# Reciprocal denominators spread by bf16 selection matmuls, with gated loads and a new order of preparation, in a fused linear-attention and MLP kernel

## The chip, the cores and the metric

The kernel runs on one core of one Trainium2 chip. The time is device microseconds (us) of that core, as the median of several executions. The kernel before takes 422 us. A profile shows one execution; its span (first to last instruction) is some 2 us below the time of that execution. The profile of the kernel before is of an execution of 419.1 us, 3 us faster than its median. TensorE's clock is granted in steps: the profile calls full speed 1.00, and half speed is 0.50.

## The reference, cut to what matters

```python
# B, H, S, D = 8, 8, 576, 64
def phi(x, c, s):                       # c, s = cos, sin of (pi/2) * position / S
    r = np.maximum(x, 0.0)
    return np.concatenate([r * c, r * s], axis=-1)
q_p, k_p = phi(q, cos_w, sin_w), phi(k, cos_w, sin_w)
kv  = einsum('bhsf,bhsd->bhfd', k_p, v)
z   = sum(k_p, axis=2)
num = einsum('bhsf,bhfd->bhsd', q_p, kv)
den = einsum('bhsf,bhf->bhs', q_p, z)[..., None] + 1e-06
attn = num / den
# tokens to rows: x is [4608, 512]
h = x @ w_in                            # 512 -> 2048
g = h / (1 + exp(-1.702 * h))
out = g @ w_out                         # 2048 -> 512
```

## The kernel before: the parts the argument touches

The MLP works on nine blocks of 512 tokens. A block has 32 units: 16 of the first matmul (`mm1`, four matmuls 128x512 and a gelu on ScalarE), then 16 of the second (`mm2`, four matmuls 128x512). Attention of the next batch (576 tokens) is slipped in between the units. Attention of one batch is: relu of q, k; transposed q times cos and sin; `kv`; `den`; a reciprocal per token and head; spreading it over the 64 partitions of the head's outputs ("the spread"); `num` times the spread reciprocals, into `xT`, which is the MLP's input.

The reciprocals `inv` lie in 32 rows of a head pair: row `32j + 16hh + 4g` holds head `2j+hh` and token segment `g`, and each value is repeated in four rows. There are two ways to spread them. Batches 0 and 1 use fp32 matmuls with a 0/1 selection matrix; batches 2 to 7 go through DRAM:

```python
def spread_dma(b):
    scr = dram.tile([2, NP, NSEG, SEG], F32, name="scr")
    for hh in range(2):
        for j in range(NP):                                  # eight small stores
            nc.gpsimd.dma_start(out=scr[hh, j], in_=s["inv"][32*j+16*hh : 32*j+16*hh+16 : 4])
    for hh in range(2):                                      # two broadcast loads
        nc.gpsimd.dma_start(out=s["invb"][hh*64:hh*64+64]..., in_=scr[hh]....to_broadcast([64, NP*S]))

def spread_pe(b, j):
    for hf in range(2):
        bps = ps.tile([128, TB], F32, name="yps", bufs=2)
        for g2 in range(2):
            nc.tensor.matmul(bps[:, ds(g2*SEG, SEG)], sel[32*j:32*j+32, 2*hf+g2]..., # fp32
                             s["inv"][32*j:32*j+32, :], start=True, stop=True)
        nc.scalar.copy(s["invb"][:, j, ds(hf*HF, HF)], bps[:, 0:HF])
...
# block i > 1; b1 = i+1 is finished here, b2 = i+2 is prepared here
for j in range(NP): work[j].append(unit_kv(b1, j))
work[6].append(unit_den(b1)); work[6].append(spread_dma(b1))
for j in range(NP):
    for hf in range(2): work[min(24 + 2*j + hf, 32)].append(unit_num(b1, j, hf))
for n, f in zip(range(8, 30), prep_all(b2)): work[n].append(f)     # relu, DMA transposes, v, trig
work[20].append(load_all(b2 + 1))
```

In the opening the queries of batch 0 are transposed by five DMA transposes, the weights' loads are issued when K has landed, and all heads of batch 0 go through each step together.

Of the kernel before, what the change touches and what calls it, by code (L numbers as in the profile page):

```python
# [15 lines left out]
EQ = mybir.AluOpType.is_equal  # L16
PSUM = bass.MemoryType.PSUM
DRAM = bass.MemoryType.DRAM
# [3 lines left out]
def kernel(  # L22
# [25 lines left out]
    dram = ctx.enter_context(tc.tile_pool(name="dram", bufs=2, space=DRAM))  # L48
# [6 lines left out]
    nc.gpsimd.memset(warm, 0.0)  # L55
    for _ in range(56):
        wps = ps.tile([128, TB], F32, name="hps", bufs=2)
        nc.tensor.matmul(wps, warm[:, 0:128], warm, start=True, stop=True)  # L58

    def load(src, b, name):  # L60
        t = one.tile([128, 2560], F32, name=name)
        nc.sync.dma_start(
            out=t[:, 0:2048].rearrange("p (h e) -> p h e", h=H),
            in_=src[b, :, 0:512, :].rearrange("h (p c) d -> p h (c d)", c=4))
        nc.sync.dma_start(  # L65
            out=t[0:64, 2048:2560].rearrange("p (h d) -> p h d", h=H),
            in_=src[b, :, 512:576, :].rearrange("h p d -> p h d"))
        return t

    def chunk(t, c):  # L70
        if c < 4:
            return t[:, 0:2048].rearrange("p (j hh c d) -> p c j hh d", hh=2, c=4, d=D)[:, c]
        return t[0:64, 2048:2560].rearrange("p (j hh d) -> p j hh d", hh=2, d=D)

    def slots(t):
        return t[:, 0:2048].rearrange("p (h c d) -> p h c d", c=4, d=D)

    state = {b: {} for b in range(B)}
    for name, src in (("qf", q), ("kf", k), ("vf", v)):
        state[0][name] = load(src, 0, name)  # L80
# [7 lines left out]
    eps = const.tile([128, 1], F32)  # L88
    nc.vector.memset(eps, 1e-6)
# [5 lines left out]
    nc.gpsimd.iota(col_i[:, 512:576], pattern=[[1, 64]], base=512, channel_multiplier=0)  # L95
    pos_f = const.tile([128, 5], F32)
    nc.vector.tensor_copy(pos_f, pos_i)
    col_f = tpool.tile([128, S], F32)
    nc.vector.tensor_copy(col_f, col_i)
    sinw = const.tile([128, 5], F32)  # L100
# [9 lines left out]
    nc.vector.memset(mask_z, 0.0)  # L110
    for hh in range(2):
        nc.vector.memset(mask_n[hh * 64:hh * 64 + 64, :, hh * 64:hh * 64 + 64], 1.0)
        for s in range(NSEG):
            nc.vector.memset(mask_z[hh * 64:hh * 64 + 64, s, hh, s, :], 1.0)
    sel_i = tpool.tile([128, NSEG, 2, 64], I32)
    sel = const.tile([128, NSEG, 2, 64], F32)
# [3 lines left out]
    nc.vector.tensor_scalar(sel, sel_i, 0.0, None, op0=EQ)  # L120

    tmp.close()
    gpool = ctx.enter_context(tc.tile_pool(name="gpool", bufs=19))
    ypool = ctx.enter_context(tc.tile_pool(name="ypool", bufs=3))

    krs, vts = [], []
    for i in range(2):
        kr = one.tile([128, 5, NP, 128], BF16, name=f"kr{i}")
        vt = one.tile([128, 5, NP, VW], BF16, name=f"vt{i}")
        nc.gpsimd.memset(kr[64:128, 4], 0.0)  # L130
        nc.gpsimd.memset(vt[64:128, 4], 0.0)
        for c in range(5):
            np_ = 128 if c < 4 else 64
            for cs, w in enumerate((cosw, sinw)):
                nc.gpsimd.tensor_copy(
                    vt[:np_, c, :, 256 + cs:257 + cs],
                    w[:np_, c:c + 1].unsqueeze(1).to_broadcast([np_, NP, 1]))
        krs.append(kr)
        vts.append(vt)
# [8 lines left out]
    def prep_q(b):  # L148
        s = state[b]
        qn = one.tile([128, 5, H, D], BF16, name="qn")  # L150
        s["qTr"] = one.tile([128, NP, S], BF16, name="qTr")
        if b == 0:
            for c in range(4):
                nc.vector.tensor_scalar(qn[:, c], slots(s["qf"])[:, :, c], 0.0, None, op0=MAX)
        else:
            nc.vector.tensor_scalar(qn[:, 0:4].rearrange("p c h d -> p h c d"), slots(s["qf"]), 0.0, None, op0=MAX)
        nc.vector.tensor_scalar(qn[0:64, 4].rearrange("p h d -> p (h d)"), s["qf"][0:64, 2048:2560], 0.0, None, op0=MAX)
        for c in range(5):
            np_ = 128 if c < 4 else 64
            nc.sync.dma_start_transpose(out=s["qTr"][:, :, c * 128:c * 128 + np_],  # L160
                                        in_=qn[:np_, c].rearrange("p h d -> p (h d)"))

    def prep_k(b):
        s = state[b]
        s["kr"] = kr = krs[b % 2]
        if b == 0:
            nc.scalar.activation(kr[:, 0:4].rearrange("p c j (hh d) -> p (j hh) c d", hh=2), slots(s["kf"]), AF.Relu)
            nc.scalar.activation(kr[0:64, 4].rearrange("p j e -> p (j e)"), s["kf"][0:64, 2048:2560], AF.Relu)
        else:
            for c2 in range(2):  # L170
                nc.vector.tensor_scalar(
                    kr[:, 2 * c2:2 * c2 + 2].rearrange("p c j (hh d) -> p (j hh) c d", hh=2),
                    slots(s["kf"])[:, :, 2 * c2:2 * c2 + 2], 0.0, None, op0=MAX)
            nc.vector.tensor_scalar(kr[0:64, 4].rearrange("p j e -> p (j e)"), s["kf"][0:64, 2048:2560], 0.0, None,
                                    op0=MAX)

    def prep_v(b, c):
        s = state[b]
        s["vt"] = vt = vts[b % 2]
        np_ = 128 if c < 4 else 64  # L180
        for cs, w in enumerate((cosw, sinw)):
            o = vt[:np_, c, :, cs * 128:cs * 128 + 128].rearrange("p j (hh d) -> p j hh d", hh=2)
            if b == 0 and cs == 1 and c in (1, 2, 3):
                nc.scalar.activation(o, chunk(s["vf"], c), AF.Identity, scale=w[:np_, c:c + 1])
            else:
                nc.vector.tensor_scalar(o, chunk(s["vf"], c), w[:np_, c:c + 1], None, op0=MUL)  # L186

    def prep_trig(b, j):
        s = state[b]
        if j == 0:  # L190
            s["qT"] = two.tile([128, NP, 2, S], BF16, name="qT")
        for cs in range(2):
            nc.vector.tensor_tensor(s["qT"][:, j, cs, :], s["qTr"][:, j, :], trig[:, cs, :], op=MUL)  # L193


    def unit_kv(b, j):
        s = state[b]
        kv_ps = ps.tile([128, VW], F32, name="kv_ps")
        for c in range(5):
            nc.tensor.matmul(kv_ps, s["kr"][:, c, j, :], s["vt"][:, c, j, :],  # L200
                             start=(c == 0), stop=(c == 4))
        kvs = two.tile([128, 2, 128], BF16, name="kvs", bufs=6)
        zs = two.tile([128, 2, NSEG, 32], BF16, name="zs", bufs=5)
# [7 lines left out]
    def unit_den(b):  # L211

        s = state[b]
        den_ps = ps.tile([128, SEG], F32, name="den_ps")
        for g in range(NSEG):
            for cs in range(2):
                for j in range(NP):
                    nc.tensor.matmul(den_ps[32 * j:32 * j + 32, :], s["zs"][j][:, cs, g, :],  # L218
                                     s["qT"][:, j, cs, ds(g * SEG, SEG)],
                                     start=(g == 0 and cs == 0), stop=(g == NSEG - 1 and cs == 1))  # L220
        den = two.tile([128, SEG], F32, name="den", bufs=1)
        nc.scalar.activation(den, den_ps, AF.Identity, bias=eps)  # L222
        inv = two.tile([128, SEG], F32, name="inv", bufs=1)
        nc.vector.reciprocal(inv, den)  # L224
        s["inv"] = inv
        s["invb"] = two.tile([128, NP, S], F32, name="invb", bufs=1)

    def spread_dma(b):
        s = state[b]
        scr = dram.tile([2, NP, NSEG, SEG], F32, name="scr")  # L230
        for hh in range(2):
            for j in range(NP):
                nc.gpsimd.dma_start(out=scr[hh, j], in_=s["inv"][32 * j + 16 * hh:32 * j + 16 * hh + 16:4])  # L233
        for hh in range(2):
            nc.gpsimd.dma_start(
                out=s["invb"][hh * 64:hh * 64 + 64].rearrange("p j s -> p (j s)"),
                in_=scr[hh].rearrange("j g s -> (j g s)").unsqueeze(0).to_broadcast([64, NP * S]))

    def spread_pe(b, j):
        s = state[b]  # L240
        for hf in range(2):
            bps = ps.tile([128, TB], F32, name="yps", bufs=2)
            for g2 in range(2):
                nc.tensor.matmul(bps[:, ds(g2 * SEG, SEG)],  # L244
                                 sel[32 * j:32 * j + 32, 2 * hf + g2].rearrange("p hh d -> p (hh d)"),
                                 s["inv"][32 * j:32 * j + 32, :], start=True, stop=True)
            nc.scalar.copy(s["invb"][:, j, ds(hf * HF, HF)], bps[:, 0:HF])  # L247

    def unit_num(b, j, hf):
        s = state[b]  # L250
        num_ps = ps.tile([128, HF], F32, name="num_ps", bufs=2)
        for cs in range(2):
            nc.tensor.matmul(num_ps, s["kvs"][j][:, cs, :], s["qT"][:, j, cs, ds(hf * HF, HF)],  # L253
                             start=(cs == 0), stop=(cs == 1))
        nc.vector.tensor_tensor(xT[:, j, ds(b * S + hf * HF, HF)], num_ps,  # L255
                                s["invb"][:, j, ds(hf * HF, HF)], op=MUL)
# [65 lines left out]
    for c in range(5):  # L322
        prep_v(0, c)
# [90 lines left out]
```

## Time and profile before

| stage (first MLP matmul to first MLP matmul) | us |
|---|---|
| opening, up to block 0's first MLP matmul | 52.4 |
| blocks 0, 1, 2, 3, 4, 5, 6 | 46.1, 53.5, 45.2, 44.4, 43.7, 38.3, 32.8 |
| blocks 7, 8 (no attention left) and the tail | 60.8 |

The borders are read from the timeline of TensorE.

The page's first part, of the kernel before: busy time of each engine, share of the span, instructions.

```profile
PE 339.3 (81%) x1785; PEld 166.3 (40%) x1816; DVE 142.5 (34%) x334; ACT 124.8 (30%) x215; POOL 73.6 (18%) x106
```

TensorE looks nearly full here. By stage it is not. The window table of the kernel before follows: stretch, its length, busy time of each engine with its number of instructions, granted TensorE clock, mean share of the DMA engines and GB/s.

```profile
core 0: us, PE busy (x) PEld busy (x) DVE busy (x) ACT busy (x) POOL busy (x), PEclk, DMA share, GB/s
0.00:52.40 52.40, 34.07 (x156) 18.72 (x158) 19.39 (x54) 10.97 (x19) 16.99 (x46) 0.68 1.06 227
...
98.50:152.00 53.50, 35.24 (x192) 16.77 (x195) 26.54 (x62) 11.90 (x21) 8.75 (x10) 0.82 0.75 187
...
197.30:241.70 44.40, 34.43 (x195) 16.63 (x197) 17.59 (x40) 12.31 (x22) 10.71 (x10) 0.88 0.57 144
...
323.60:356.50 32.90, 32.69 (x194) 16.14 (x196) 7.74 (x17) 12.18 (x22) 5.00 (x10) 1.00 0.30 69
```

Block 3 (third row) and block 6 (fourth) do the same TensorE work, 195 and 194 matmuls. Block 6 needs 32.9 us and is full; block 3 takes 44.4 us and leaves TensorE 10 us idle. The waits of the kernel before (who waited for whom: us in all, times, longest) name the cause:

```profile
DVE xT L255 <- DMA invb<-scr: 62.0, 5, 16.6
...
PE num_ps L253 <- DVE xT L255: 50.3, 5, 18.1
```

The chain of waits through block 3 (start, us, what) shows the way of the reciprocals:

```profile
207.36 1.06 DVE inv L224
...
208.71 8.43 POOL scr L233 x6
...
217.88 6.80 DMA scr<-inv
...
225.23 8.65 DMA invb<-scr
...
234.01 0.47 DVE xT L255
...
234.52 0.64 PE num_ps L253 x2
```

The reciprocal is done at 208.4, and num goes on at 234.5: 26.1 us for one trip through DRAM. When its num buffers are full TensorE stands still, and the MLP matmuls that come later in its program stand with it: in the last 7.2 us of the wait it ran not one matmul (columns as in the window table).

```profile
227.30:234.50 7.20, 0.00 (x0) 0.00 (x0) 0.49 (x2) 0.00 (x0) 0.00 (x0) 0.50 1.08 273
```

### The profile page before, as it was taken

The numbers are of one execution on the slowest core, as the hardware profiler recorded it, in microseconds if no ns is written. First come the engines' busy times: TensorE is split into PE (matmuls) and PEld (weight loads), VectorE is DVE, ScalarE is ACT, GpSimd is POOL, SyncE is SP. The second block draws the span as 40 slices with busy tenths as digits, with TensorE's granted clock in tenths as the row PEclk, the third lists the DMA queues.
The fourth block names the chain that finished last, engine by engine and source line by source line (L and its number), as shares of the span: only waits on it lengthen the run. The fifth ranks groups of instructions, "written<-read, shape, count | busy, mean of one in ns | idle before, by whom it ended". The sixth has DMA issues, their size and how long they took to land.

```text
span 417.3 us, 4663 instructions
## 1 busy us (share of the span) xinstructions
PE 339.3 (81%) x1785; PEld 166.3 (40%) x1816; DVE 142.5 (34%) x334; ACT 124.8 (30%) x215; POOL 73.6 (18%) x106
## 2 busy tenths in 40 slices
PE   8606999989992099927995599739996999999995
PEld 3204734455441044413542254315443544444442
DVE  4433281146543075603471237214732302100000
ACT  2401254123610015301450036102610451541631
POOL 9700000000016003600090007200540040000000
PEclk9955579986998589977998699959998999999998
DMA  8999839301767960794049812991162143001113
GB/s 236 235 224 231 215 66 310 97 27 33 215 174 184 245 160 13 173 289 114 27 88 306 191 27 58 277 236 43 40 140 70 25 101 85 32 6 71 26 27 75
DMA packets 69590, 54.16 MB, mean 130 GB/s; under 512 B 35328, under 2 KB 64192, under 8 KB 68800
## 3 DMA queue, kind: packets, MB, share of 16 engines
q1 hardware_dynamic: 57344, 33.04, 31.2%
q0 software_dynamic: 6720, 11.39, 13.3%
q10 hardware_dynamic: 5504, 9.44, 8.3%
q8 instruction: 14, 0.23, 0.2%
q14 instruction: 8, 0.07, 0.1%
HBM read 43.78 MB, written 9.55 MB: 128 GB/s over the span
## 4 chain that ended last, share of the span: by engine, by line
PE 58%; DMA 22%; POOL 9%; DVE 4%; issue 3%; ACT 2%; SPq 1%; ACTq 1%; DVEq 0%; POOLq 0%
PE hps L264 22%; PE yps L293 20%; DMA invb<-scr 11%; POOL scr L233 9%; DMA scr<-inv 6%; PE kv_ps L200 5%; PE num_ps L253 5%; PE yps L244 4%; DMA qTr<-qn 3%; DMA vf<-in_v_dram 2%; DVE inv L224 2%; PE den_ps L218 1%; DVE qT L193 1%; SPq L65 1%; ACT den L222 1%
## 5 line engine op out<-in xcount | busy, mean ns | idle before, releaser
L293 PE MATMUL yps<-w_out_sb,g 128*128 128x512 bf16 x562 | 138.1, 391 | 0.6
L264 PE MATMUL hps<-xT,w_in_sb 128*128 128x512 bf16 x559 | 131.8, 385 | 2.5 <-ACT g L267 1.3
L267 ACT ACTIVATE g<-hps 128x512 bf16<-128x512 f32 x144 | 85.6, 597 | 59.7 <-PE hps L264 56.9
L233 POOL DMA_DIRECT2D scr<-inv x48 | 50.3, 1056 | 244.3 <-DVE inv L224 244.3
L264 PEld LDWEIGHTS <-w_in_sb 128*128 128x128 bf16 x576 | 56.9, 99 | 65.6 <-issue 6.1
L293 PEld LDWEIGHTS <-g 128*128 128x128 bf16 x576 | 58.0, 101 | 62.5 <-issue 4.2
L297 ACT COPY ysb<-yps 128x512 f32<-128x512 f32 x36 | 21.1, 586 | 174.8 <-PE yps L293 163.4
L253 PE MATMUL num_ps<-qT,kvs 128*128 128x288 bf16 x128 | 30.6, 342 | 50.4 <-DVE xT L255 50.3
L255 DVE TENSOR_TENSOR xT<-num_ps,invb 128x288 bf16<-128x288 f32 x64 | 28.7, 456 | 118.7 <-DMA invb<-scr 62.0
L253 PEld LDWEIGHTS <-kvs 128*128 128x128 bf16 x128 | 13.3, 109 | 67.3 <-issue 56.6
L200 PE MATMUL kv_ps<-vt,kr 128*128 128x258 bf16 x160 | 25.4, 289 | 14.9 <-DVE kvs L207 12.5
L193 DVE TENSOR_TENSOR qT<-qTr,trig 128x576 bf16<-128x576 bf16 x64 | 24.5, 452 | 21.7 <-DMA qTr<-qn 17.3
L204 DVE TENSOR_TENSOR zs<-kv_ps,mask_z 128x256 bf16<-128x256 f32 x32 | 13.6, 424 | 44.2 <-PE kv_ps L200 44.2
L200 PEld LDWEIGHTS <-kr 128*128 128x128 bf16 x160 | 14.2, 101 | 31.0 <-DVE kvs L207 23.8
L186 DVE TENSOR_SCALAR vt<-vf,cosw 128x512 bf16<-128x512 f32 (+1 forms) x40 | 19.9, 503 | 6.1 <-DMA vf<-in_v_dram 6.1
L244 PE MATMUL yps<-inv,sel 32*128 32x144 f32 x64 | 16.2, 420 | 3.1 <-DVE inv L224 3.1
L186 DVE TENSOR_SCALAR vt<-vf,sinw 128x512 bf16<-128x512 f32 (+1 forms) x37 | 17.9, 483 | 0.0
L244 PEld LDWEIGHTS yps<-inv,sel 32*128 32x128 f32 x64 | 13.7, 290 | 6.2 <-DVE inv L224 3.6
L58 PE MATMUL hps<-warm 128*128 128x512 bf16 x56 | 14.2, 419 | 1.3 <-POOL warm L55 1.3
L224 DVE RECIPROCAL inv<-den 128x144 f32<-128x144 f32 x8 | 8.4, 1053 | 20.1 <-ACT den L222 20.1
L207 DVE TENSOR_TENSOR kvs<-kv_ps,mask_n 128x256 bf16<-128x256 f32 x32 | 13.3, 414 | 0.0
L247 ACT COPY invb<-yps 128x288 f32<-128x288 f32 x16 | 6.4, 398 | 18.5 <-PE yps L244 18.3
(45 smaller groups left out, 82.0 us busy)
## 6 DMA issues: line engine op xcount, KB each, us to landing
qf<-in_q_dram SPq DMA_DIRECT2D x8, 1024.0 KB, 6.3
kf<-in_k_dram SPq DMA_DIRECT2D x8, 1024.0 KB, 14.2
vf<-in_v_dram SPq DMA_DIRECT2D x8, 1024.0 KB, 13.5
invb<-scr POOLq DMA_DIRECT2D x12, 576.0 KB, 9.3
out_dram<-ysb ACTq DMA_DIRECT2D x40, 128.0 KB, 2.4
out_dram<-ysb ACTq DMA_DIRECT2D x16, 256.0 KB, 2.4
w_in_sb<-in_moe_w_in_dram POOLq DMA_DIRECT2D x4, 512.0 KB, 10.7
w_out_sb<-in_moe_w_out_dram POOLq DMA_DIRECT2D x4, 512.0 KB, 23.7
```

The lines of the kernel that those rows point to most:

```text
L186: nc.vector.tensor_scalar(o, chunk(s["vf"], c), w[:np_, c:c + 1], None, op0=MUL)
L193: nc.vector.tensor_tensor(s["qT"][:, j, cs, :], s["qTr"][:, j, :], trig[:, cs, :], op=MUL)
L200: nc.tensor.matmul(kv_ps, s["kr"][:, c, j, :], s["vt"][:, c, j, :], start=(c == 0), stop=(c == 4))
L224: nc.vector.reciprocal(inv, den)
L233: nc.gpsimd.dma_start(out=scr[hh, j], in_=s["inv"][32 * j + 16 * hh:32 * j + 16 * hh + 16:4])
L244: nc.tensor.matmul(bps[:, ds(g2 * SEG, SEG)], sel[32 * j:32 * j + 32, 2 * hf + g2].rearrange("p hh d -> p (hh d)"), s["inv"][32 * j:32 * j ...
L253: nc.tensor.matmul(num_ps, s["kvs"][j][:, cs, :], s["qT"][:, j, cs, ds(hf * HF, HF)], start=(cs == 0), stop=(cs == 1))
L255: nc.vector.tensor_tensor(xT[:, j, ds(b * S + hf * HF, HF)], num_ps, s["invb"][:, j, ds(hf * HF, HF)], op=MUL)
L264: nc.tensor.matmul(hps, w_in_sb[:, kc, ds(fc * 128, 128)], xT[:, kc, ds(i * TB, TB)], start=(kc == 0), stop=(kc == NP - 1))
L267: nc.scalar.activation(g, hps, AF.Gelu_apprx_sigmoid)
L293: nc.tensor.matmul(yps, gT[fc][:, ds(t * 128, 128)], w_out_sb[:, fc, :], start=(fc == 0), stop=(fc == FC - 1))
L297: nc.scalar.copy(ysb, yps)
```

## The change

The intent is fourfold. The spread is done on TensorE for every batch, at bf16 cost: a reciprocal is split into three bf16 parts that sum to it, and since each value has four rows, rows 0, 1, 2 of the four can hold the three parts, and the selection matrix sums them. Batch i+1 is prepared and finished within block i. The weights, batch 1 and batch 2 are loaded in a set order, by one-element copies that hold a queue until something has landed. In the opening the transposes go to TensorE, and batch 0 is done in two halves of four heads.

```diff
-    nc.vector.tensor_scalar(sel, sel_i, 0.0, None, op0=EQ)              # fp32, one row per value
+    nc.vector.tensor_scalar(sel_a, sel_i, 0.0, None, op0=GE)            # bf16, rows 0..2 of each four
+    nc.vector.scalar_tensor_tensor(sel, sel_i, 2.0, sel_a, op0=LE, op1=MUL)
...
+        nc.vector.reciprocal(inv[r], den[r])
+        nc.vector.tensor_copy(p0[r], inv[r])                                       # bf16 part 0
+        nc.vector.scalar_tensor_tensor(d1[r], p0[r], part1[r], inv[r], op0=MUL, op1=ADD)
+        nc.vector.tensor_copy(p1[r], d1[r])                                        # bf16 part 1
+        nc.vector.scalar_tensor_tensor(comb[r], p1[r], part2[r], d1[r], op0=MUL, op1=ADD)
...
-    def spread_dma(b): ...
+    def unit_spread(b, j, on=None):            # as spread_pe, with bf16 sel and comb; for all batches
...
+    transpose_pe(0, 0)                         # opening and batch 1: PE transposes, PSUM, times trig
...
+    nc.gpsimd.tensor_copy(junk[:, 0:1], s0["vf"][0:1, 0:1])             # w_in waits for V
+    ...w_in...
+    nc.sync.dma_start(out=junk[:, 8:9], in_=w_in_sb[0:1, 0, 1534:1536]...) # batch 1 waits for w_in
+    load_all(1)
+    nc.gpsimd.tensor_copy(junk[:, 1:2], state[1]["vf"][0:1, 0:1])       # w_out waits for batch 1
+    ...w_out...
+    for jh in range(2):                        # batch 0 in halves
+        ...prep_v, unit_kv x2, unit_den(0, 2*jh, 2*jh+2), warmup(4), unit_spread/unit_num x2
...
+        # block i, b = i+1, k0 = 4 if i == 0 else 0
+        at(0, load_all, b + 1)                 # i > 0
+        at(k0, prep_q, b, 0, 4); ...; at(k0 + 1, transpose_dma, b)      # i > 0
+        ... prep_k, prep_v, prep_trig at k0+2 .. k0+12
+        at(k0 + 14 + j, unit_kv, b, j); at(k0 + 19, unit_den, b)
+        at(k0 + 22 + 2*j, unit_spread, b, j); at(min(32, k0 + 23 + 2*j), unit_num, b, j)
```

PSUM tiles of the attention become one pool of three (`at`), and one buffer for the transposes (`att`). Output stores stay on ScalarE's queue.

## The prediction

> **What bounds the kernel now.** TensorE's busy share (81% on the page) hides stages. From the chain of waits, cut at the first matmul of each MLP block (nine blocks of 512 tokens):
>
> - Opening, before block 0's first MLP matmul: 52.4 us.
> - Blocks 0 to 6: 46.1, 53.8, 45.3, 44.4, 43.7, 38.1, 32.9 us.
> - Blocks 7 and 8, which prepare no attention, with the tail: 60.7 us.
>
> Block 6 has its reciprocals in time and runs dense: 32.9 us at clock 1.00 (stage table). That bounds an attention block. Blocks 1 to 5 are 225 us instead of 165. The waits say why: TensorE waited for num's evacuation (DVE xT) 5 times, 50.3 us, and DVE for the invb DMA 62.0 us. The chain there reads reciprocal, eight POOL issues (about 8.5 us), scr landing (up to 7), invb landing (8 to 11). After each stop the granted clock falls; stage means are 0.82 to 0.89. The Trainium skill ("TensorE: Matmul & The Clock Gate", What's actually happening) gives half rate after an idle window of about 3.4 us; this trace agrees, with clock 0.50 from 20 to 56 us.
>
> **What the change does, costed.**
>
> - Spread in blocks 1 to 5 moves from DRAM to TensorE: 16 matmuls 32x144 per batch. The fp32 form took 1.2 us per four spreads warm, 2.2 us cold, in two passes: bf16 should need one, estimate 1.2 to 1.8 us per block. ACT gains eight 0.40 us copies, DVE about 1.2 us of splitting: both are under half busy, so free. Block estimate 32.9+1.5+0.3 = 34.7 us, so five blocks cost 173 us: -52 us. The main gain, all on the critical path.
> - Block 6 gains the spread: +1.8.
> - Opening: the first transposes go from DMA (10.8 us beside the weights, ending at 26.5) to TensorE; weights wait for V; heads are taken in halves. Estimated: transposes end near 18 us (one PSUM buffer, about 2.2 us a pair), half one of kv, den, reciprocal, split, spread, num ends near 31, half two, serial behind it on DVE, near 43. TensorE stays at half clock. -9.5 us.
> - Block 0: spread of batch 1 is interleaved, not bunched at the end (11 us), but 20 transposes (2 us) and a last spread-to-num wait (1.5 us) come in: about 41, -5.
> - Blocks 7, 8, tail: the same.
> - Loads now precede transposes in queue order, but each load is released by the preparation two batches earlier, so I expect no transpose behind bulk loads.
>
> Span: 43+41+208+61 = 353, rounded up; the timed median lies 4 us above the span: **355 us**, range 346 to 368. Chances: faster by over 2% 0.97, within 2% 0.02, slower 0.01.
>
> **What would show it.** TensorE's wait for xT nearly gone; no scr or invb DMA; blocks 1 to 6 each 33.5 to 36 us at clock near 1.0; spread group about 0.1 us spacing; first MLP matmul at 39 to 47 us, still at clock 0.5; TensorE above 80% of the chain.
>
> **What would make it wrong.** Out-stores share completion semaphores with loads: an ACT store issue that waits for a late load would hold invb copies, then TensorE. Transposes behind 3.5 MB of loads would stall DVE before kv by 5 us or more a block. W_out, loaded after batch 1, may be late for block 0. 300 us of dense matmuls might be throttled (the dense end, 90 us, shows 0.96 to 1.00).

## More of the kernel before

The runs were made on several chips; the kernel before ran beside each of them and had medians of 422.0 to 424.9 us, so kernels of different rounds are best compared by their ratio to it.

## The result, and the profile after

The changed kernel takes 353.12 us (351.89 to 356.59, 4 runs); the kernel before, on the same chip, 421.97 us. The ratio is 0.838, with a 95% interval of 0.831 to 0.845. A ratio here and below is the mean time of one kernel's fast runs over that of the other's of the same rounds, so it is not quite the ratio of the quoted medians.

| stage | before | predicted | after |
|---|---|---|---|
| opening | 52.4 | 43 | 38.1 |
| block 0 | 46.1 | 41 | 39.2 |
| blocks 1 to 5, sum | 225.1 | 173 | 175.6 |
| block 6 | 32.8 | 34.7 | 35.9 |
| blocks 7, 8, tail | 60.8 | 61 | 61.3 |
| span | 417.3 | 353 | 350.0 |

The window table of the changed kernel, for the opening and blocks 0, 1, 4 and 6 (columns as before):

```profile
0.00:38.07 38.07, 27.61 (x136) 12.75 (x138) 23.31 (x66) 11.28 (x22) 11.64 (x42) 0.72 1.01 259
38.07:77.30 39.23, 38.04 (x228) 18.42 (x232) 19.24 (x46) 15.95 (x29) 4.73 (x5) 0.97 0.93 241
77.30:112.00 34.70, 34.21 (x210) 17.05 (x212) 20.56 (x51) 14.11 (x27) 0.00 (x0) 1.00 0.51 147
...
182.50:218.20 35.70, 34.30 (x210) 17.07 (x213) 18.94 (x47) 14.59 (x28) 0.00 (x0) 1.00 0.51 146
...
252.90:288.80 35.90, 34.39 (x210) 17.05 (x212) 18.05 (x44) 14.59 (x28) 0.00 (x0) 1.00 0.20 47
```

The blocks are full, at clock 1.00. They hold 210 matmuls instead of 195. The waits of TensorE in the changed kernel show that the 50.3 us are gone:

```profile
PE hps L320 <- ACT g L323: 4.1, 5, 1.0
PE at L298 <- DVE den L289: 3.1, 9, 1.1
...
PE at L310 <- ACT invb L302: 0.5, 2, 0.2
```

The largest wait now is for a gelu, 4.1 us in 5 times; it is why blocks 2, 4 and 6 take 35.7 to 35.9 us and blocks 1, 3, 5 only 34.7 to 34.8. Of the chain that ended last, TensorE has:

```profile
PE 83%; DVE 9%; ACT 3%; ACTq 2%; issue 2%; DVEq 0%
```

So the sum came out as predicted. Whether the reasons were right is another question: the change does at least five things at once. The next section takes them apart.

### The profile page after: what moved, and what is told of

Read it like the earlier page. It is cut to its first block, busy times and chain, and to the rows that moved or that the text cites. A ratio compares the mean times of both kernels' runs of the same rounds, so it can differ in the third digit from the quotient of the medians.

```text
span 350.0 us, 4868 instructions
## 1 busy us (share of the span) xinstructions
PE 326.8 (93%) x1861; PEld 158.4 (45%) x1896; DVE 157.1 (45%) x388; ACT 138.9 (40%) x259; POOL 16.4 (5%) x45
## 4 chain that ended last, share of the span: by engine, by line
PE 83%; DVE 9%; ACT 3%; ACTq 2%; issue 2%; DVEq 0%
PE hps L320 34%; PE yps L348 30%; PE at L259 5%; PE at L310 5%; PE at L298 3%; DVE den L285 3%; PE hps L72 2%; PE at L276 2%; ACTq L354 2%; PE att L208 1%; DVE vt L252 1%; ACT ysb L352 1%; DVE den L289 1%; DVE den L287 1%; DVE qT L212 1%
## 5 line engine op out<-in xcount | busy, mean ns | idle before, releaser
L323 ACT ACTIVATE g<-hps 128x512 bf16<-128x512 f32 x144 | 85.5, 597 | 49.9 <-PE hps L320 49.5
L312 DVE TENSOR_TENSOR xT<-at,invb 128x288 bf16<-128x288 f32 x64 | 26.7, 453 | 54.3 <-PE at L310 52.3
L302 ACT COPY invb<-at 128x288 f32<-128x288 f32 x64 | 22.6, 402 | 70.1 <-PE at L298 69.6
L262 DVE TENSOR_TENSOR zs<-at,mask_z 128x256 bf16<-128x256 f32 x32 | 13.6, 425 | 33.5 <-PE at L259 33.5
L259 PE MATMUL at<-vt,kr 128*128 128x258 bf16 x160 | 25.5, 289 | 2.7 <-DVE vt L252 1.3
L225 DVE TENSOR_TENSOR qT<-qTr,trig 128x576 bf16<-128x576 bf16 x48 | 18.2, 452 | 15.3 <-DMA qTr<-qn 15.3
L310 PE MATMUL at<-qT,kvs 128*128 128x288 bf16 x128 | 22.5, 297 | 0.7 <-ACT invb L302 0.5
L252 DVE TENSOR_SCALAR vt<-vf,cosw 128x512 bf16<-128x512 f32 (+3 forms) x45 | 19.6, 447 | 0.0
L252 DVE TENSOR_SCALAR vt<-vf,sinw 128x512 bf16<-128x512 f32 (+3 forms) x39 | 18.1, 463 | 0.0
L298 PE MATMUL at<-den,sel 32*128 32x144 bf16 x128 | 14.1, 229 | 3.3 <-DVE den L289 3.1
L265 DVE TENSOR_TENSOR kvs<-at,mask_n 128x256 bf16<-128x256 f32 x32 | 13.3, 414 | 0.0
L196 DVE TENSOR_SCALAR qn<-qf 128x1024 bf16<-128x1024 f32 x15 | 10.4, 696 | 0.0
```

The costliest lines, as they stand in the source:

```text
L225: nc.vector.tensor_tensor(s["qT"][:, j, cs, :], s["qTr"][:, j, :], trig[:, cs, :], op=MUL)
L252: nc.vector.tensor_scalar(o, i, w, None, op0=MUL)
L259: nc.tensor.matmul(kv_ps[:, 0:VW], kr[:, c, j, :], vt[:, c, j, :], start=(c == 0), stop=(c == 4))
L298: nc.tensor.matmul(bps[:, ds(g2 * SEG, SEG)], sel[32 * j:32 * j + 32, 2 * hf + g2].rearrange("p hh d -> p (hh d)"), s["comb"][32 * j:32 * ...
L302: nc.scalar.copy(invb, bps[:, 0:HF])
L310: nc.tensor.matmul(num_ps[:, 0:HF], s["kvs"][j][:, cs, :], s["qT"][:, j, cs, ds(hf * HF, HF)], start=(cs == 0), stop=(cs == 1))
```

## The experiments

All eleven kernels gave correct results. "Changed kernel" is the one of 353.1 us. Stage times come from each run's one profile.

### e1_fp32_select: is it the place of the spread, or the bf16 parts?

```diff
-    sel: bf16, rows 0..2 of each four        -    split into p0, p1, comb
+    sel: fp32, EQ 0                          +    s["comb"] = inv
```

> The changed kernel, but the spread multiplies the fp32 reciprocals by an fp32 selection matrix; the bf16 split is gone. Theory A (only the place of the spread matters, the bf16 parts are a refinement): the four spread matmuls of a head pair cost 1.2 us warm as they did before instead of 0.42, so about 3 us a block over seven blocks, and some 4 us in the half-clock opening, where 2.6 us of splitting goes away: about 378 us, still clearly faster than before. Rival B (the bf16 parts are what makes the spread on TensorE pay): near or above 410 us.

Measured: 378.1 us (377.7 to 378.5), ratio 0.891. Blocks 1 to 6 take 37.8 to 38.8 us, on average 3.0 us more than in the changed kernel, and the opening 42.7. One head pair's spread in a late block, first with fp32 (this run), then with bf16 (changed kernel), from the timelines:

```profile
223.26 1.24 PE L292 MATMUL at<-den,sel 32*128 32x144 f32 x8
```

```profile
209.30 0.42 PE L298 MATMUL at<-den,sel 32*128 32x144 bf16 x4
```

Each fp32 matmul is two in the trace, and four of them cost 1.24 us instead of 0.42 us. Theory A's 378 us is met, and rival B's 410 us is out. The bf16 parts are worth 25 us, about a third of the whole gain, but the kernel is faster than before without them.

### e2_before_pe_spread: the new place alone, in the old order

```diff
-                work[k0 + 6].append(lambda: spread_dma(b1))
+            for j in range(NP):
+                work[k0 + 7 + j].append(lambda j=j: spread_pe(b1, j))
```

> The kernel before, with one change: batches 2 to 7 use its own fp32 selection matmuls for the spread, one head pair after each of the four MLP units behind the reciprocal. Theory A (the DRAM round trip of the reciprocals held TensorE at num in blocks 1 to 5): these blocks fall from a mean of 45 us to about 38, block 6 rises from 32.9 to about 38, total about 390 us. Rival C (the new order of preparation and loads is what made the loop dense): 412 us or more, blocks 1 to 5 still above 42 us.

Measured: 413.8 us, but from 407.9 to 422.5 in four runs; two of them are over 1.5% above the fastest, and no ratio is given. The profile is of the fastest. The total is nearer to rival C's 412 us than to theory A's 390; the blocks tell them apart. Blocks 2 to 6 take 38.8 to 39.4 us, as theory A said, where rival C had blocks above 42. Block 1 misses: 50.7 us. There the spread lies among the second matmuls and shares their two PSUM buffers, TensorE first waits 1.2 us for the reciprocal (it is busy for 1.7 of the 3.4 us from 123.8 on), and then its clock falls and stays down. The window table of that stretch:

```profile
130.00:135.00 5.00, 4.53 (x14) 2.87 (x15) 0.33 (x1) 1.38 (x3) 0.00 (x0) 0.50 0.46 102
135.00:140.00 5.00, 4.45 (x14) 2.47 (x14) 0.00 (x0) 1.19 (x3) 0.00 (x0) 0.50 1.04 272
```

TensorE is 89% to 91% busy here, and still at half clock; the record shows 0.50 from 127.2 to 144.3 us. The opening of the kernel before has the same picture: from 38.96 to 52.40 us, with fp32 selections and num in turn, TensorE is busy for 13.21 of 13.44 us, and the clock is 0.50 throughout. Yet in blocks 1 to 6 of e1 fp32 selections of 1.24 us each stand among the MLP matmuls, and the clock stays at 1.00. Why so busy an engine is not given its full clock back is not settled by these runs. The miss against 390 us lies in block 1 (some 13 us) and in blocks that are 1 us longer than estimated. In this block the bunched spread cost more than its matmuls. The slower runs have no profile, so what varies by 15 us from run to run is not known.

### e3_before_two_queues: a shorter trip through DRAM

```diff
-                nc.gpsimd.dma_start(out=scr[hh, j],
+                (nc.gpsimd if j % 2 else nc.sync).dma_start(out=scr[hh, j],
```

> The kernel before, round trip kept, but four of its eight stores of reciprocals are issued by SyncE and four by GpSimd, side by side. That takes about 4 us out of the chain from reciprocal to invb and leaves TensorE's work alone. Theory A (the block ends when the round trip ends): each of blocks 1 to 5 is about 4 us shorter, total about 402 us. Rival C: no change beyond 3 us.

Measured: 404.6 us (403.3 to 408.3), ratio 0.955 (0.948 to 0.963). Blocks 2 to 5 fall from 45.2, 44.4, 43.7, 38.3 to 39.5, 39.7, 40.8, 34.5 us; block 1 does not (55.4). In block 3, reciprocal to xT takes 19.7 us instead of 25.6 (its chain has GpSimd's four stores still at 7.2 us), and the block is 4.7 us shorter. TensorE's work is the same, so in these blocks the trip sets most of the block's time. Rival C's "no change" is out for them. It is one changed line, and it brings 19 to 20 us.

### e4_after_dram_spread: the new order with the old place

From block 1 on the reciprocals of the changed kernel go through DRAM again:

```diff
+            if i > 0:
+                at(k0 + 19, spread_dma, b)
...
-                at(k0 + 22 + 2 * j, unit_spread, b, j)
+                if i == 0: at(k0 + 22 + 2 * j, unit_spread, b, j)
```

> The changed kernel with its opening, its loads and its order of preparation, but from block 1 on the reciprocals go through DRAM as before. Theory A: the reciprocal is ready about 22 us into a block and the round trip takes about 24 us, so num waits until about 46 us and a block takes about 53 us: total about 465 us, slower than the kernel before, since its late preparation relies on the short spread. Rival C (order and loads bring the gain): under 400 us.

Measured: 407.7 us (2 runs), ratio 0.961 (0.952 to 0.970), which is classed as unclear. Both expectations miss: the blocks take 42.8 to 44.7 us, neither 53 nor below 37. The chain in one of them, in the same columns as block 3's of the kernel before:

```profile
233.10 1.06 DVE den L286
...
234.45 2.95 POOL scr L316 x6
...
237.92 2.31 DMA scr<-den
...
240.79 6.10 DMA invb<-scr
...
247.01 0.47 DVE xT L329
```

From the end of the reciprocal (234.2) to xT takes 12.8 us, half of the 25.6 us in block 3 before. The issue of the eight stores takes 4.0 instead of 9.7 us, their landing 2.3 instead of 6.8. The final landing takes 6.1 instead of 8.7 us. The issue of the eight stores, in the kernel before and in this run:

```profile
208.71 9.66 POOL L233 DMA_DIRECT2D scr<-inv  x8 [27.79 <-DVE inv L224]
```

```profile
234.45 3.97 POOL L316 DMA_DIRECT2D scr<-den  x8 [37.73 <-DVE den L287]
```

In the kernel before, SyncE issues five DMA transposes and then 3.5 MB of loads while the trip is under way; in the new order their issue is over by then. That is the likely reason for the slower landings, 7 of the 12.8 us; no run changes the queues' traffic alone. The other 5.7 us are issue time of GpSimd, and they go with DVE rather than with the queues. In each of blocks 1 to 5 of the kernel before, and of e3, one single store takes 3.9 to 5.8 us to issue (most take 0.5), and it ends within 0.3 us of the end of an unbroken run of tensor_scalar operations in which DVE prepares the next batch (in block 3 DVE's run is from 208.3 to 215.3 us, and the store's issue from 209.6 to 215.4). In block 6 of the kernel before, where DVE prepares nothing, the eight take 4.0 us, and in e4, where that preparation is over by then, also 4.0. That DVE's run holds the issue up fits all of these, but was not tested by itself. So my 24 us for the trip was not a property of the trip: half of it was its company. What remains, theory A's core, is that with the late reciprocal of the new order even the short trip costs each block 9 us against the spread on TensorE.

The runs together give the sum of blocks 1 to 6, each from one profile (stages rounded to 0.1 us):

| sum of blocks 1 to 6, us | old order | new order |
|---|---|---|
| spread through DRAM | 257.9 (before) | 264.3 (e4) |
| spread on TensorE, fp32 | 245.4 (e2) | 229.7 (e1) |
| spread on TensorE, bf16 | not run | 211.5 (changed) |

The order alone is worth nothing while the reciprocals go through DRAM (it costs 6.4 us); with the spread on TensorE it is worth 15.7, of which 12.8 is block 1. The parts of the change need each other. The figure for e2 is the weakest: its profile is of the fastest of four runs that lie 15 us apart, so the split between place and order holds for that execution only. "New order" also includes the other pools of PSUM buffers and the spread's new position among the units; these were not tested apart.

### e5_open_dma_transpose: what shortens the opening?

```diff
-    transpose_pe(0, 0); transpose_pe(0, 1); ...; transpose_pe(0, 2); transpose_pe(0, 3)
+    transpose_dma(0); ...; prep_trig(0, j) for all j
```

> The changed kernel, but batch 0's queries are transposed by five DMA transposes as before; all else of the opening is kept. Theory A (the transposes on TensorE are a large part of the shorter opening): qT of batch 0 is complete near 23 us instead of 15.1, the first MLP matmul comes 6 to 9 us later, total about 360 us. Rival D (the weights that wait for V are what shortened the opening, the transposes are then off the chain): within 2 us of 353.

Measured: 367.0 us (363.7 to 367.7), ratio 0.866. The first MLP matmul comes at 50.4 us instead of 38.1. The multiplication by cos and sin, from the timelines of this run and of the changed kernel (its last pair):

```profile
25.38 3.04 DVE L225 TENSOR_TENSOR qT<-qTr,trig 128x576 bf16<-128x576 bf16 x8 [15.80 <-DMA qTr<-qn]
```

```profile
14.29 0.82 DVE L212 TENSOR_TENSOR qT<-att,trig 128x576 bf16<-128x576 bf16 x2 [0.86 <-PE att L208]
```

DVE waits 15.8 us for the DMA transposes, and qT is complete at 28.4 us instead of 15.1. Without this one part the opening is 12.4 us longer, and its whole gain was 14.3. The expected 6 to 9 us were too few.

### e8_no_gates: what do the gates of the loads do?

The three one-element copies are taken out; the weights are issued as soon as GpSimd is free, batch 1 right behind batch 0.

```diff
-    nc.gpsimd.tensor_copy(junk[:, 0:1], s0["vf"][0:1, 0:1])
-    nc.sync.dma_start(out=junk[:, 8:9], in_=w_in_sb[0:1, 0, 1534:1536].bitcast(F32))
-    nc.gpsimd.tensor_copy(junk[:, 1:2], state[1]["vf"][0:1, 0:1])
```

> The changed kernel, but the three one-element copies that hold back the weights and batch 1 are gone: both weight matrices are issued as soon as GpSimd is free, near 9 us, and batch 1 right after batch 0. Theory A: V and the second heads of K share the queues with 4 MB of weights, V lands some 4 us later and the second half some 6 us later, so the first MLP matmul comes 4 to 8 us later: about 359 us. Rival G (the gates do nothing for the time): within 1.5 us of 353.

Measured: 353.8 us (352.4 to 354.7), ratio 0.837: the same as the changed kernel, as rival G said. The opening even ends at 36.7 us, and block 0 takes 42.9 instead of 39.2. The gates move time between two stages and gain none.

### e6_open_whole: are the halves of batch 0 worth it?

```diff
-    for jh in range(2): prep_v, unit_kv, unit_den(0, 2*jh, 2*jh+2), warmup(4), unit_spread, unit_num
+    prep_v (all heads); unit_kv(0, 0..3); unit_den(0); warmup(4); unit_spread, unit_num for 0..3
```

> The changed kernel, but batch 0 goes through kv, den, reciprocal, split, spread and num once with all eight heads instead of twice with four. Theory A (the second half only begins on DVE when the first has ended, and the chain of den, reciprocal and split is paid twice, about 4.5 us with its matmuls): the first MLP matmul comes at about 34 us instead of 38, total about 349 us. Rival E (halves hide the later landing of the second heads): the same or slower, 353 to 357 us.

Measured: 353.8 us (351.5 to 355.5), ratio 0.836: no gain. But theory A was right about the opening, which now ends at 31.9 us, 6.2 earlier. Block 0 gives all of it back: 48.2 us instead of 39.2. TensorE's waits in this run, and how long w_out took to land after its issue at 37.6 to 39.8 us:

```profile
PE yps L348 <- DMA w_out_sb<-in_moe_w_out_dram: 4.3, 2, 3.5
...
DMA to landing us min/median/max: 9.2/14.3/19.7
```

The second matmuls of block 0 arrive before their weights. The stop also brings the clock down to 0.50 from 54.4 to 64.7 us. The DMA engines are full until about 68 us in this run (their share is 1.1 or more in each window of 4 us up to there), and w_out shares them with batch 2 and, from 46 us on, with batch 3, which nobody needs before blocks 1 and 2. Rival E's total of 353 to 357 us is met, but not for its reason.

### e9_whole_gate: load batch 2 behind w_out

```diff
+                at(28, lambda: nc.sync.dma_start(out=junk[:, 10:11],
+                       in_=w_out_sb[0:1, FC - 1, 510:512].bitcast(F32)))   # batch 2 waits for w_out
                 at(28, load_all, b + 1)
```

> The run with batch 0 in one pass, with one more gate: the load of batch 2 waits for the last byte of w_out. That run began the MLP at 31.9 us but its block 0 took 48.2 us, with TensorE standing still for w_out. Theory H (block 0 is bound by the transfers: the queues are full until about 68 us and w_out shares them with batch 2, which nobody needs before 70 us): w_out lands near 48 us, block 0 takes 39 to 41 us, total 343 to 346 us. Rival J (the half-clock start of the MLP or the missing overlap in the opening makes block 0 long): block 0 stays above 45 us and the total above 350 us.

This run has batch 0 in one pass, as e6, and the gate is its only change against e6. Measured: 347.8 us (347.2 to 348.3), ratio 0.820 (0.817 to 0.824), against 0.836 for e6. Block 0 takes 41.3 us. The landing of w_out, issued at the same times as in the run before:

```profile
DMA to landing us min/median/max: 5.8/9.1/11.8
```

The wait for w_out is gone. Theory H holds. Its total of 343 to 346 us is missed by 2 us; w_out has landed at 51.6 us, not near 48, and block 0 is 0.3 us above the 39 to 41 us expected. This gate pays, where the three of the change together did not.

### e7_stores_pool: the output stores leave ScalarE

```diff
-                nc.scalar.dma_start(out=out[row...], in_=ysb[...])
+                nc.gpsimd.dma_start(out=out[row...], in_=ysb[...])
```

> The changed kernel, but the stores of the output are issued by GpSimd, which is idle after the opening, instead of ScalarE. Theory A: blocks 2, 4 and 6 are about 1 us longer than 1, 3 and 5 because a store issue of ScalarE stands between the last ysb copy and the first gelu; without it TensorE's wait for gelu falls from 4.1 us to about 1, total about 350 us. Rival F (the issue only fills idle time of ScalarE, and software-issued stores end later): 353 to 355 us.

Measured: 350.4 us (350.1 to 354.5), ratio 0.831 (0.826 to 0.835); the interval overlaps that of the changed kernel, so the time alone does not part them. The stages do: blocks 1 to 6 take 34.6 to 34.8 us, the alternation is gone, and TensorE's wait for gelu falls from 4.1 to 0.7 us. The tail grows from 61.3 to 63.5 us. In the profiled execution, the slowest of the six, block 0 took 44.7 us with 3.6 us of waiting for w_out: the hazard that e6 brought out is there in other openings too.

### e10_whole_gate_pool: together

e9, with the stores on GpSimd in all blocks but the last, and the transposes ahead of the loads in the queue:

```diff
-                nc.scalar.dma_start(out=out[row
+                (nc.gpsimd if i < NBLK - 1 else nc.scalar).dma_start(out=out[row
-            if i > 0: at(0, load_all, b + 1) if b + 1 < B else None
                 at(k0 + 1, transpose_dma, b)
+                if b + 1 < B: at(k0 + 2, load_all, b + 1)
```

> The same with two more changes: the output stores of all blocks but the last are issued by GpSimd, and from block 1 on the DMA transposes of a batch stand before the loads of the next one in the queue. The stores alone took blocks 2, 4 and 6 from 35.7 to 34.6 us and cost 2 us at the end, which the last block's ScalarE issue should save. Theory H: 31.9 + 39 + 6 x 34.6 + 61.3 = 340 us of span, 343 us timed, and block-to-block differences below 0.3 us. If GpSimd's stores disturb the late loads of block 0, block 0 is above 42 us.

Measured: 342.0 us (341.0 to 343.0), ratio 0.807 (0.803 to 0.811). Block 0 takes 39.5 us, blocks 1 to 6 take 34.8 and five times 34.6, the tail 60.2, near theory H's 39, 34.6 and 61.3. This beats both kernels of the study. Which of the two additions gave how much beyond e9 was not tested apart.

### e11_warm_open: keep TensorE warm in the opening

```diff
     transpose_pe(0, 0)
+    warmup(2)              # likewise behind pairs 1 and 2; warmup(8) behind pair 3
...
     unit_den(0)
-    warmup(4)
+    warmup(10)
```

> The fastest run so far (342.0 us), with more matmuls on the zero tile to fill TensorE's idle time in the opening: two behind each of the first three pairs' transposes, eight behind the last, and ten instead of four behind den. Theory K (the half clock from 13.5 to 20 us and from 27 us into block 0 is a real cost of the opening and of the first matmuls of block 0): the clock stays at 1.00 from 6 us on, first MLP matmul at 29 to 30.5 us instead of 31.8, block 0 shorter by 1 to 2 us, total 338 to 340 us. Rival L (the opening is bound by DVE and the transfers, the extra matmuls only get in the way): 341.5 to 344 us.

Measured: 340.7 us (339.9 to 341.0), ratio 0.803 (0.799 to 0.808). The interval overlaps e10's, so a gain of 0.4% is likely and not proved. The clock stays at 1.00 from 6.5 to 27.0 us, and the first MLP matmul comes at 30.1 us, 1.7 earlier. Block 0 takes 41.0 instead of 39.5:

```profile
PE yps L348 <- DMA w_out_sb<-in_moe_w_out_dram: 1.0, 1, 1.0
```

w_out is late again by a little. Neither expectation is met in full: the total is just above theory K's 338 to 340 us and below rival L's, and block 0 became longer, not shorter. Block 0 ends at 71.1 us against 71.3 in e10, so most of the earlier start was lost again. That the opening and block 0 together are now close to what the transfers allow is likely, not tested.

## Why the prediction was right, and where its reasons were not

- **The total.** 353.1 us against 355, inside the range of 346 to 368. The profiled span is 350.0 against 353. So close a hit is in part luck: the opening and block 0 came out 6.7 us shorter than predicted, blocks 1 to 6 and the tail 4.1 us longer. The 4 us from span to timed value were 2.1 in this run; 353 plus 4 would also have been 357, not 355.
- **The bound.** Right. Blocks 1 to 6 run at clock 1.00 and 34.7 to 35.9 us, inside the stated 33.5 to 36; TensorE has 83% of the chain; its wait for xT is gone.
- **The main gain.** "Five blocks cost 173 us: -52 us": they cost 175.6, so -49.5. The mechanism, TensorE standing at num while reciprocals travel, is shown from two sides: e3 shortens the trip and four of the five blocks shrink, e4 puts it back and they grow by 9 us. A detail was misread: the stage clocks of 0.82 to 0.89 hold for blocks 1 to 4, block 5 had 0.96.
- **Whose gain it is.** The prediction put all of it to the spread on TensorE at bf16 cost and gave the order no effect. The table says that the place alone gives 12.5 us in the old order, place and order 28.2, and the bf16 parts 18.2 more. Not wrong as a sum, but a reader who took over only the place would get about a quarter, and by the spread of e2's runs perhaps less.
- **The trip's length.** Read from the trace of before, and right there. Carried over to another schedule, in e4's expectation, it was twice too long.
- **The opening.** The mis-sized term: 38.1 us against 43, and just before the 39 to 47 us named as the sign. Transposes and trig took 1.5 us a pair and ended at 15.1, not 18 with 2.2 a pair. A DVE product that reads bf16 from PSUM took 450 ns, as from SBUF (452). Each half took 11 to 12 us instead of 12 to 13. Of the three measures I named for the opening, the transposes carry it (e5), the gates give nothing (e8), and the halves cost 6 us of opening that block 0 hid (e6).
- **The spread's cost.** The estimate of 1.2 to 1.8 us a block was right: four times 0.42 us.
- **Not foreseen.** The 1 us in every second block from a store issue between ysb and gelu (e7).
- **The warnings.** "W_out may be late for block 0" was the one that mattered. It does not show in the profile of the changed kernel, but in e6, e7 and e11 TensorE waited 4.3, 3.6 and 1.0 us for w_out. Late loads holding store issues, transposes behind bulk loads and a throttle under 300 us of dense matmuls did not show in the profile of the changed kernel.

The page "TensorE: Matmul & The Clock Gate" of the Trainium skill (What's actually happening) says that the clock has two states, half and full, and changes after windows of about 3.4 us. The runs agree: in the clock records only 1.00 and 0.50 occur, and the stretches at half clock within a run last 3.4, 6.8, 10.2, 13.7, 17.1, 20.5, 30.7 or 37.5 us, whole multiples of 3.41. The agreement that the prediction found in the opening is partial: TensorE was idle for 10.8 us there (19.4 to 30.3 us), but the half clock lasts until 56.5 us, over the 13.4 us in which it was nearly always busy (e2). The page "DMA: Bandwidth & Descriptors" (Queues, rings and completion order) says that an engine takes turns between queues that have work. That fits e6 and e9: w_out on GpSimd's queue took up to 19.7 us beside the batches on SyncE's, and at most 11.8 us without. The page "VectorE: DVE Perf Modes" lists a tensor-tensor product with any PSUM operand at the slowest rate (The perf-mode tier table), while its section Why PSUM operands drop a tier has only fp32 fall that far; the measured 450 and 452 ns side with the second.

## What to carry to other kernels

A round trip through DRAM in the middle of a pipeline cost 25.6 us in one schedule of this kernel and 12.8 in another: read its length in the schedule in which it will run, and look at what runs beside it, on the queues and on DVE. When an opening is made shorter, look at what the first full stage waits for next; a gain of 6 us vanished because weights shared the queues with batches that nobody needed yet, and one gate in the right place brought it back. When a change does five things, a table of "which part, in which order" on a few runs shows more than the total, which came out right for partly the wrong reasons.

## What the Trainium skill lacked or had wrong

- "TensorE: Matmul & The Clock Gate": it gives an idle window, or small idle gaps between groups of matmuls, as the reason for half clock. In e2, TensorE was 89% and 91% busy in two stretches of 5 us, with fp32 selection matmuls and second MLP matmuls in turn, and stayed at 0.50 for 17.1 us; in the opening of the kernel before it was busy for 13.21 of 13.44 us at 0.50. What share of activity counts as busy, and whether small fp32 matmuls count, is not said.
- "FP8 and Floating Point Precision" (TensorE Precision Notes) says that true fp32 takes four passes. Here each fp32 matmul of 32x144 shows as two matmuls, and four of them took 1.24 us against 0.42 us with bf16, a factor of 3.0.
- "VectorE: DVE Perf Modes" (The perf-mode tier table) has a bf16 tensor-tensor product at half the rate when an operand is in PSUM, which its own section Why PSUM operands drop a tier does not say for bf16. Here 128x576 took 450 ns with one operand in PSUM and 452 ns with both in SBUF.
- "DMA: Bandwidth & Descriptors" (Anatomy of one DMA): a transfer costs a fixed 2.0 us or so plus its bytes, with no term for other traffic. After their issue the same eight small stores and the last broadcast load took 6.8 and 8.7 us to land in the kernel before, beside transposes and loads, and 2.3 and 6.1 us in e4. The page describes how queues take turns and names a longer HBM latency under load, but gives no figure for a transfer beside other queues' traffic.
